# A second MLP layer on four column groups, stores of 16 rows, and five early loads issued by ScalarE

## The chip, the core and the metric

The kernel runs on one core of one Trainium2 chip. The metric is device time in microseconds; lower is better. Times are medians of several executions. Ratios are the mean time of one kernel's runs over that of the kernel before in the same rounds, so they are not quite the ratio of the medians quoted. A profile shows one execution, whose span (first to last instruction) is some 2 us shorter than its time. In profiles, PE is TensorE's matmuls, PEld its weight loads, DVE VectorE, ACT ScalarE, POOL GpSimd; SPq and ACTq are the DMA requests that SyncE and ScalarE issue.

## The reference

One decoding step of a transformer block for 8 batches: a conditioned layer norm, attention over a cache, and an MLP.

```python
B, Sq, D = (8, 1, 512);  Hq, Hkv, Sk, Dh = (32, 8, 8192, 128);  F = 1792      # bfloat16
mod = (silu(c) @ w_mod).reshape(B, 6, 1, D)          # sa, ca, ga, sb, cb, gb
h = layernorm(x) * (1 + ca) + sa
x = x + ga * (softmax(q(h) @ k_cache.T / sqrt(Dh)) @ v_cache @ wo)
h = layernorm(x) * (1 + cb) + sb
x = x + gb * (relu(h @ w1 + b1) ** 2 @ w2 + b2)
```

The two caches are 268 MB of the 284 MB that are read. All else is small.

## The kernel before

Keys and values come in 64 units of 4 MB (each two heads of one batch) through a ring of four slots. For each batch the order is units k0 to k3, then v0 to v3. A unit is requested when its slot has been read. All large loads are issued by SyncE, in one queue:

```python
d_wm = dma("sync", s_wm, ...)            # w_mod, 3 MB, ring slot 2
d_wq = dma("sync", s_wq, ...)            # wq, 4 MB, ring slot 3
...
load(0)
load(1)
dma("sync", s_bb, ...)                   # three small biases
...
d_wo = dma("sync", s_wo, ...)            # wo, 4 MB in rows of 4 KB
load(2)                                  # waits until w_mod has been read
load(3)                                  # waits until wq has been read
```

The request for unit 4 (the first values) also waits for wo, the output projection's weight, to have landed:

```python
def load(n):
    ...
    dep = [released.get(s), d_wo if n == NSLOT else None]
```

That wait guards the projection with wo. The projection stands inside the loop over batches and has no wait of its own for wo: it relies on some unit, asked for after wo landed, having been waited for earlier.

The end of the kernel, after the last values: first MLP layer, second layer with W2 stationary and 8 columns moving, scaling, transposing by matmul, copy, two stores of 8 rows of 512 B from neighbouring partitions:

```python
for f in range(FT):                      # 14 x 4 matmuls
    for k in range(KT):
        t = matmul(yT_ps[:, k, :], W2v[:, f, k * 128:(k + 1) * 128], hidT[:, f, :])
...
k_y2 = vector.tensor_tensor(y2T, yT_ps, mod(5), ALU.mult)
for cc in (1, 0):
    ...                                  # 2 matmuls by IDENT, then a copy into out_sb[rows, :]
    dma(("sync", "scalar")[cc], ..., outf[:, 256 * cc:256 * (cc + 1)], out_sb[rows, :])
```

Of the kernel before, what the change touches and what calls it, by code (L numbers as in the profile page):

```python
# [168 lines left out]
def bass_adaLN_cond__gqa_block_cached__dense_activation_squared_relu__decode_kernel(  # L169
# [10 lines left out]
    NSLOT = 4  # L180
# [6 lines left out]
    with ExitStack() as es:  # L187
# [25 lines left out]
        SEL = sb("SEL", [128, 4, 8], BF16)  # L213
# [13 lines left out]
        SELB = sb("SELB", [4, 4, B], BF16)  # L227
        SELP = sb("SELP", [128, B], FP32)
        x1T = sb("x1T", [128, KT, B], BF16)
# [4 lines left out]

        KF = KTb[:, :, :, :].rearrange("p a t r -> p (a t r)")
# [10 lines left out]
        EYEB = KF[:, 4544:4576].rearrange("p (g b) -> p g b", g=4)  # L246
# [5 lines left out]
        hidT = KF[:, 2560:2560 + FT * B].rearrange("p (f b) -> p f b", f=FT)  # L252
        out_sb = KF[:, 2048:2304]
# [4 lines left out]
        y2T = KF[:, 0:KT * B].rearrange("p (k b) -> p k b", k=KT)  # L258
# [38 lines left out]
        pool(lambda e: e.memset(IDF8[:], 0.0))  # L297
# [4 lines left out]
        pool(lambda e: e.memset(R4m[:], 0.0))  # L302
        pool(lambda e: e.memset(SEL[:], 0.0))
# [12 lines left out]
        t = select(IDF8[:], [[-1, 8]], 0, 1, 1.0, NE, t)  # L316
        k_id = t
        pool(lambda e: e.memset(KF[:, 4096:4096 + 64 * KT], 0.0))
        pool(lambda e: e.memset(EYE[:], 0.0))
        t = pool(lambda e: e.memset(EYEB[:], 0.0))  # L320
        t = select(EYE[:], [[-32, 4], [-1, B]], 0, 1, 1.0, NE, t)
        t = k_eye = select(EYEB[:], [[-32, 4], [-1, B]], 0, 1, 1.0, NE, t)
# [3 lines left out]
        for d in (-96, -64, -32, 0, 32, 64, 96):  # L326
            t = select(R4[:], [[-1, 128]], -d, 1, 1.0, NE, t)
        t = select(Qmask[:], [[-32, 4]], 0, 1, 0.0, GE, t)
        t = select(Qmask[:], [[32, 4]], 31, -1, 0.0, GE, t)
        for d in (0, 32, 64, 96):  # L330
            t = select(R4m[:], [[-1, 32]], -d, 1, 0.5, NE, t)

        for i in range(4):
            for cg in range(4):
                for half in range(2):
                    t = select(SEL[:, i, 4 * half:4 * half + 4], [[-1, 4]], -(32 * cg + 8 * i + 4 * half), 1,
                               1.0, NE, t)
# [5 lines left out]
        t = select(SELB[:], [[-1, 4], [0, B]], 0, 1, 1.0, NE, t)  # L343
# [11 lines left out]
        def load(n):  # L355
            kv, b, p = units[n]
            s = n % NSLOT
            src = (A_k_cache if kv == "k" else A_v_cache)[b, 2 * p:2 * p + 2]
            src = src.rearrange("g s d -> (g s d)").rearrange("(p f) -> p f", p=128)
            dep = [released.get(s), d_wo if n == NSLOT else None]  # L360
            if units[n] == last:
                t0, toks = 0, []
                for i, t1 in enumerate(CH):
                    toks.append(dma("sync", s_last[i - 1] if i else s_ring[s], lambda e, a=t0 * DH, z=t1 * DH: e.dma_start(
                        RING[:, s, a:z], src[:, a:z]), dep))
                    t0 = t1
                loaded[n] = toks
            else:
                loaded[n] = dma("sync", s_ring[s], lambda e: e.dma_start(slot(s), src), dep)
# [9 lines left out]
        k_csT = op("vector", lambda e: e.tensor_copy(csT[:, :, 0:B], csT_ps), [t, k_eye])  # L379
# [34 lines left out]
        k_mr1 = op("scalar", lambda e: e.activation(mod_r[:, 1, :], bank(1), ACT.Copy), [t])  # L414
# [8 lines left out]
        k_haT = op("vector", lambda e: e.tensor_tensor(haT[:, :, 0:B], tmpT[:], mod(0), ALU.add), [t])  # L423
        for i in range(KT):
# [7 lines left out]
               op("scalar", lambda e: e.activation(q_r[:, 1, :], bank(3), ACT.Copy), [t])]  # L432
        for u in range(2):
            for i in range(4):
                t = op("tensor", lambda e, u=u, i=i: e.matmul(
                    QT_ps[:, u, :, i, :], q_r[:, u, DH * i:DH * (i + 1)], EYEB[:, :, :]), [k_q[u]])
# [12 lines left out]
        k_cb1 = op("vector", lambda e: e.tensor_scalar(cb1[:], mod(4), 1.0, None, ALU.add))  # L449

# [3 lines left out]
        load(1)  # L454
        dma("sync", s_bb, lambda e: e.dma_start(
            b1_row[0:3, :], B_b1[0:128 * F2].rearrange("(o f) -> o f", o=3)), [k_brow])
        dma("sync", s_bb, lambda e: e.dma_start(
            b1_row[3:4, 0:256], B_b1[128 * F2:F].rearrange("(o f) -> o f", o=1)))
        d_bb = dma("sync", s_bb, lambda e: e.dma_start(b2_row, B_b2.rearrange("(o f) -> o f", o=4)))
        d_wo = dma("sync", s_wo, lambda e: e.dma_start(  # L460
# [56 lines left out]
        yT_ps = bank(2)[:, 0:KT * B].rearrange("p (k b) -> p k b", k=KT)  # L517

        def permute(pP, q0, q1, dst, deps, fill, then=None):
            n = q1 - q0  # L520
            for j in range(4):
                t = t_act = op("tensor", lambda e, j=j: e.matmul(
                    pP[:, j, 0:64 * n].rearrange("p (h x) -> p h x", h=2), PERM[:, j, :, :].rearrange("p h m -> p (h m)"),
                    oTn_p[:, :, q0:q1, :, :].rearrange("p h q r b -> p h (q r b)"), start=True, stop=True), deps)
            if fill:
                t_act = pe_stream(fill, 4)
# [3 lines left out]
            for hl in range(REP):  # L530
# [3 lines left out]
                if hl % 2:  # L534
                    toks.append(op("scalar", lambda e, dst=dst_h, frm=frm: e.activation(dst, frm, ACT.Copy), [t_act]))  # L535
# [13 lines left out]
        for b in range(B):  # L549
# [76 lines left out]
            for p in range(NP):  # L626
# [16 lines left out]
                if p == NP - 1:  # L643
                    proj_done = project(permute(
                        PS[:, 5:7, :].rearrange("p a (j c) -> p (a j) c", c=256), 0, 3, oPe,
                        [norm_last, k_all] + stg_free + hold, 3))
                    values(0, 16, 28)
                    Pg.at = "post" if lastb else (b, "b")
                if not lastu:
# [9 lines left out]
                    for i in range(4):  # L659
                        t = op("tensor", lambda e, i=i, osb=osb, oT_ps=oT_ps: e.matmul(  # L660
                            oT_ps, osb[:, i * 128:(i + 1) * 128], SEL[:, i, :], start=(i == 0), stop=(i == 3)),
# [12 lines left out]
                else:  # L674
# [29 lines left out]
                    for hh, (f0, n, a, z) in enumerate(((0, 4, 0, 2), (0, 4, 2, 3), (4, 2, 3, 4))):  # L704
                        for j in range(n):
                            op("tensor", lambda e, hh=min(hh, 1), f0=f0 + j, j=j, n=n, a=a, z=z: e.matmul(
                                hT_ps[hh][:, f0:f0 + 4 * (z - a - 1) + 1:4, 1, :], brow(j, n), SELB[:, a:z, :],
                                start=(f0 == 0), stop=False, skip_group_check=True), [d_bb, s_bank_free[min(hh, 1)]])
                    op("tensor", lambda e: e.matmul(
                        yT_ps, b2_row, SELB[:, :, :], start=True, stop=False, skip_group_check=True),  # L710
# [6 lines left out]
                    for i in range(4):  # L717
                        op("tensor", lambda e, i=i: e.matmul(
                            oT_ps, osb[:, i * 128:(i + 1) * 128], SEL[:, i, :], start=False, stop=False,
# [6 lines left out]
                    k_oP = permute(bank(6)[:, 0:256].rearrange("p (j c) -> p j c", c=64), 3, 4, oP, [t], 0,  # L726
# [10 lines left out]
        k_x1 = op("vector", lambda e: e.tensor_tensor(x1T[:], t1T[:], xT[:], ALU.add), [t])  # L737
        mean_ps = bank(3)[:, 0:B]
        for k in range(KT):
            t = op("tensor", lambda e, k=k: e.matmul(mean_ps, ONESMB[:, :], x1T[:, k, :], start=(k == 0),  # L740
                                                    stop=(k == KT - 1)), [k_x1])
        bc = lambda ap: ap.unsqueeze(1).to_broadcast([128, KT, B])
        t = op("vector", lambda e: e.tensor_tensor(xcT[:], x1T[:], bc(mean_ps), ALU.subtract), [t])
# [8 lines left out]
        for k in range(KT):  # L752
            if k == KT - 1:
                t = op("tensor", lambda e: e.matmul(var_ps, ONESM[:, :], sqs[:]), [k_sqs])
                t = op("scalar", lambda e: e.activation(std2[:], var_ps, ACT.Sqrt, bias=epst[:, 0:1]), [t])
                k_rstd = op("vector", lambda e: e.reciprocal(rstd2[:], std2[:]), [t])
            for f in range(FT):
                t = op("tensor", lambda e, f=f, k=k: e.matmul(
                    hT_ps[f // 8][:, f % 8, :, :], wcol(k, f), hbT[:, k, :, :], start=False, stop=(k == KT - 1),
                    skip_group_check=True), [k_hb, k_sb, d_w1[k // (KT - 1)]])  # L760
                if k == KT - 1 and f in (7, FT - 1):
                    hh = f // 8
                    fs = slice(8 * hh, f + 1)
                    t = op("vector", lambda e, hh=hh, fs=fs: e.tensor_tensor(
                        rT[:, fs, :], hT_ps[hh][:, :, 0, :], rsb(fs.stop - fs.start), ALU.mult), [t, k_rstd])
                    t = op("vector", lambda e, hh=hh, fs=fs: e.tensor_tensor(
                        rT[:, fs, :], rT[:, fs, :], hT_ps[hh][:, :, 1, :], ALU.add), [t])
                    k_sq.append(op("vector", lambda e, fs=fs: e.scalar_tensor_tensor(
                        hidT[:, fs, :], rT[:, fs, :], 0.0, rT[:, fs, :], ALU.max, ALU.mult), [t]))
        o_ps = bank(4)[:, 0:256]  # L770
        for f in range(FT):
            for k in range(KT):
                t = op("tensor", lambda e, f=f, k=k: e.matmul(  # L773
                    yT_ps[:, k, :], W2v[:, f, k * 128:(k + 1) * 128], hidT[:, f, :],
                    start=False, stop=(f == FT - 1), skip_group_check=True), [k_sq[f // 8], d_w2[f // 4]])
        for cc in range(2):
            for k in range(2):
                op("tensor", lambda e, k=k, cc=cc: e.matmul(
                    o_ps[64 * cc:64 * cc + B, 128 * k:128 * (k + 1)], x1T[:, 2 * cc + k, :], IDENT[:, :],
                    start=(k == 0), stop=False, tile_position=(0, 64 * cc), skip_group_check=True), [k_x1])  # L780
        k_y2 = op("vector", lambda e: e.tensor_tensor(y2T, yT_ps, mod(5), ALU.mult), [t])
        outf = out.rearrange("b s d -> (b s) d")
        d_o = []
        for cc in (1, 0):
            for k in range(2):
                t = op("tensor", lambda e, k=k, cc=cc: e.matmul(
                    o_ps[64 * cc:64 * cc + B, 128 * k:128 * (k + 1)], y2T[:, 2 * cc + k, :], IDENT[:, :],
# [40 lines left out]
```

## Time and profile before

| | kernel before |
|---|---|
| time | 669.41 us, median of 3 (668.55 to 670.22); 669.0 with a fourth run |
| span of the profile | 666.7 us |
| bytes read | 283.66 MB |
| busy: PE, DVE, ACT | 79%, 46%, 40% |
| one DMA queue | 99.3% of the span of 16 engines |

The prediction shows the rows of busy tenths and the queue's share. This is how the early requests look in the timeline of SyncE's queue. The columns are start and duration of the issuing instruction in us; "x2" merges neighbours, waits between them included, so such a duration is not that of one issue.

```profile
4.00 0.40 SPq L460 DMA_DIRECT2D wo_sb<-in_A_wo_dram  x1
14.86 23.69 SPq L369 DMA_DIRECT2D ring<-in_A_k_cache_dram  x2
51.38 31.83 SPq L369 DMA_DIRECT2D ring<-in_A_v_cache_dram  x4
```

### The profile page before, as it was taken

Reading aid. Unit: us, or ns where it says so; the run is one execution under the profiler, and the core shown is the slowest. Engines: PE = TensorE matmul, PEld = TensorE weight load, DVE = VectorE, ACT = ScalarE, POOL = GpSimd, SP = SyncE. Lnnn points to the kernel's source line nnn. Section 1 sums busy time; section 2 is a strip of 40 time slices with the busy share of each in tenths; the row PEclk is TensorE's granted clock in tenths of the full one; section 3 lists DMA queues with packets and bytes.
Section 4 is the critical chain, followed back from the end, with each engine's and each line's share of the span. In section 5 each row is a group of like instructions: output and inputs, shape, how many; then the busy total and the mean of one; then the engine's idle time right before and its main releaser. Section 6 shows DMA issues by size and latency. Waiting matters only on the chain.

```text
span 666.7 us, 15924 instructions
## 1 busy us (share of the span) xinstructions
PE 528.3 (79%) x7259; PEld 352.2 (53%) x7259; DVE 307.9 (46%) x587; ACT 264.3 (40%) x307; POOL 20.5 (3%) x79
## 2 busy tenths in 40 slices
PE   3494976898849987599858988499776998589887
PEld 2383732675328742477316753287424773277535
DVE  1262741466316652367415662167513673146633
ACT  2151631466115651166314661166512663146611
POOL 7400000000000000000000000000000000000000
PEclk9696998799969999699998999799997999879996
DMA  9999999999999999999999999999999999999997
GB/s 375 437 406 441 419 433 433 425 434 431 438 427 433 433 434 427 434 434 425 434 431 438 427 431 434 434 427 431 438 425 434 433 436 427 431 434 434 427 420 285
DMA packets 12189, 283.85 MB, mean 426 GB/s; under 512 B 1261, under 2 KB 1297, under 8 KB 3601
## 3 DMA queue, kind: packets, MB, share of 16 engines
q1 hardware_dynamic: 12128, 283.65, 99.3%
q8 instruction: 9, 0.15, 0.1%
q10 hardware_dynamic: 48, 0.02, 0.0%
q14 instruction: 4, 0.02, 0.0%
HBM read 283.66 MB, written 0.01 MB: 425 GB/s over the span
## 4 chain that ended last, share of the span: by engine, by line
PE 52%; DMA 38%; ACT 6%; DVE 2%; issue 1%; SPq 0%; DVEq 0%
PE PS L488 36%; DMA ring<-in_A_k_cache_dram 33%; PE PS L505 9%; ACT P_sb L582 5%; DMA ring<-in_A_v_cache_dram 4%; DMA ring<-in_A_wq_dram 2%; PE PS L636 2%; PE PS L478 1%; ACT KTb L493 1%; DVE O_sb L656 1%; PE PS L472 1%; PE PS L594 1%; DVE Pm L608 0%; PE PS L614 0%; PE PS L773 0%
## 5 line engine op out<-in xcount | busy, mean ns | idle before, releaser
L488 PE MATMUL PS<-IDENT,ring 128*128 128x128 bf16 x4096 | 267.1, 227 | 56.2 <-DMA ring<-in_A_k_cache_dram 56.2
L488 PEld LDWEIGHTS PS<-IDENT,ring 128*128 128x128 bf16 x4096 | 246.5, 102 | 104.8 <-DMA ring<-in_A_k_cache_dram 57.4
L493 ACT ACTIVATE KTb<-PS 128x1024 bf16<-128x1024 bf16 x192 | 196.5, 1024 | 236.6 <-PE PS L488 236.6
L495 DVE COPY KTb<-PS 128x1024 bf16<-128x1024 bf16 x320 | 210.0, 688 | 146.5 <-PE PS L488 144.4
L636 PE MATMUL PS<-ring,Pm 128*32 128x512 bf16 x1018 | 67.2, 409 | 24.8 <-DMA ring<-in_A_v_cache_dram 23.9
L505 PE MATMUL PS<-KTb,Qb 128*32 128x512 bf16 x1024 | 79.0, 385 | 4.5 <-ACT KTb L493 4.5
L656 DVE CAST O_sb<-PS 128x512 bf16<-128x512 f32 x31 | 21.5, 692 | 112.7 <-PE PS L636 112.7
L636 PEld LDWEIGHTS PS<-ring,Pm 128*32 128x32 bf16 x1018 | 26.5, 101 | 61.8 <-DMA ring<-in_A_v_cache_dram 33.7
L535 ACT ACTIVATE KTb<-PS 32x192 bf16<-32x192 f32 (+1 forms) x18 | 5.6, 310 | 110.0 <-PE PS L472 103.9
L582 ACT ACTIVATE P_sb<-PS,negm 128x1024 bf16<-128x1024 f32 x32 | 35.2, 1111 | 20.2 <-DVE negm L577 20.2
L478 PE MATMUL PS<-ONES 128*128 128x512 f32 x80 | 42.1, 630 | 0.0
L472 PE MATMUL PS<-IDENT 128*128 128x512 bf16 x112 | 33.4, 380 | 0.0
L594 PE MATMUL PS<-IDENT,P_sb 128*128 128x128 bf16 x256 | 19.9, 220 | 15.4 <-ACT P_sb L582 15.4
L608 DVE COPY Pm<-PS 64x512 bf16<-64x512 bf16 x48 | 20.2, 421 | 25.0 <-PE PS L594 24.5
L594 PEld LDWEIGHTS PS<-IDENT,P_sb 128*128 128x128 bf16 x256 | 14.4, 98 | 25.1 <-ACT P_sb L582 25.1
L505 PEld LDWEIGHTS PS<-KTb,Qb 128*32 128x32 bf16 x1024 | 15.4, 94 | 21.0 <-ACT KTb L493 8.5
L512 DVE TENSOR_REDUCE m<-PS 128x1 f32<-128x512 f32 x32 | 22.1, 689 | 6.6 <-PE PS L505 6.6
L660 PEld LDWEIGHTS PS<-SEL,O_sb 128*128 128x128 bf16 x124 | 5.8, 97 | 30.0 <-DVE O_sb L656 30.0
L478 PEld LDWEIGHTS PS<-ONES 128*128 128x128 f32 x80 | 12.7, 190 | 10.6 <-issue 10.6
L660 PE MATMUL PS<-SEL,O_sb 128*128 128x8 bf16 x124 | 7.8, 169 | 12.3 <-DVE O_sb L656 12.0
L472 PEld LDWEIGHTS PS<-IDENT 128*128 128x128 bf16 x112 | 9.9, 104 | 10.1 <-issue 7.2
L543 PE MATMUL PS<-wo_sb,KTb 128*32 128x512 bf16 x192 | 11.8, 380 | 3.3 <-ACT KTb L535 3.3
(134 smaller groups left out, 147.0 us busy)
## 6 DMA issues: line engine op xcount, KB each, us to landing
ring<-in_A_k_cache_dram SPq DMA_DIRECT2D x32, 4096.0 KB, 34.0
ring<-in_A_v_cache_dram SPq DMA_DIRECT2D x31, 4096.0 KB, 27.8
ring<-in_A_wq_dram SPq DMA_DIRECT2D x1, 4096.0 KB, 19.8
wo_sb<-in_A_wo_dram SPq DMA_DIRECT2D x1, 4096.0 KB, 47.3
ring<-in_w_mod_dram SPq DMA_DIRECT2D x1, 3072.0 KB, 10.5
ring<-in_A_v_cache_dram SPq DMA_DIRECT2D x1, 2048.0 KB, 22.5
ring<-in_B_w_dram SPq DMA_DIRECT2D x3, 512.0 KB, 19.2
ring<-in_B_w_dram SPq DMA_DIRECT2D x1, 1344.0 KB, 17.8
```

The costliest lines, as they stand in the source:

```text
L472: ts = [op("tensor", lambda e: e.matmul(bank(at).rearrange("p (a r) -> p a r", a=4), IDENT[:, :], rhs)) for _ in range(n)]
L478: ts = [op("tensor", lambda e: e.matmul(bank(at).rearrange("p (a r) -> p a r", a=4), ONES[:, :], rhs)) for _ in range(n)]
L488: t = op("tensor", lambda e, j=j, i=i: e.matmul(STG[j][:, i, :], src[:, 32 * k + 8 * j + i, :], IDENT[:, :], is_transpose=True), [loaded[n ...
L493: stg_free[j] = op("scalar", lambda e, j=j, dst=dst: e.activation(dst, STG[j], ACT.Copy), [t])
L495: stg_free[j] = op("vector", lambda e, j=j, dst=dst: e.tensor_copy(dst, STG[j]), [t])
L505: t = op("tensor", lambda e, hf=hf, q=q, rhs=rhs: e.matmul(PS[32 * q:32 * (q + 1), k, :], Qb[:, 2 * p + hf, :], rhs, start=(p == 0 and hf ...
L512: return op("vector", lambda e: e.tensor_reduce(m4[:, k:k + 1], bank(k), AX.X, ALU.max), [t])
L582: exps.append(op("scalar", lambda e, k=k: e.activation(P_sb[:, k, :, :, :], bank(k).rearrange("p (i x) -> p i x", i=8).unsqueeze(2).to_bro ...
L594: t = op("tensor", lambda e, k=k, i=i: e.matmul(STG[k][:, i, :], P_sb[:, k, i, :, :].rearrange("p h x -> p (h x)"), IDENT[:, :], is_transp ...
L608: done.append(op("vector", lambda e, dst=dst, frm=frm: e.tensor_copy(dst, frm), [t, k_pm]))
L636: t = op("tensor", lambda e, m=m, cg=cg, p=p, vt=vt, Obank=Obank: e.matmul(Obank[32 * cg:32 * (cg + 1), :], lhs[:, p, 32 * m:32 * m + 32], ...
L656: t = op("vector", lambda e, osb=osb, Obank=Obank: e.tensor_copy(osb, Obank), [t])
```

## The change

Intent: shorten the ending, by putting the output rows in the layout of the store without transposes; clear ScalarE of the early copies so that it can issue five early loads; and shorten the setup on GpSimd. The diff, cut to its core:

```diff
-            dep = [released.get(s), d_wo if n == NSLOT else None]
+            dep = [released.get(s), d_wo if n == 2 * NSLOT - 1 else None, k_wq if eng == "scalar" else None]
...
-        k_mr1 = op("scalar", lambda e: e.activation(mod_r[:, 1, :], bank(1), ACT.Copy), [t])
+        k_mr1 = op("vector", lambda e: e.tensor_copy(mod_r[:, 1, :], bank(1)), [t])
...
         load(0)
-        load(1)
-        dma("sync", s_bb, ...)                       # three biases
-        d_wo = dma("sync", s_wo, ...)
+        load(1, "scalar")
+        dma("scalar", s_bb, ...)                     # three biases
+        d_wo = dma("scalar", s_wo, ...)
...
-                    proj_done = project(permute(..., 3))
+                    t = permute(...)
                     values(0, 16, 28)
+                    proj_done = project(t)
...
-                    yT_ps[:, k, :], W2v[:, f, k * 128:(k + 1) * 128], hidT[:, f, :],
+                    y_ps[32 * k:32 * (k + 1), :], hidw[:, f].rearrange("p b r -> p (b r)"), W2v[:, f, k * 128:(k + 1) * 128],
+                    ..., tile_position=(0, 32 * k), ...
...
-        k_y2 = ...mult...; two transposes and a copy for each half; two stores of 8 rows of 512 B
+        t = op("vector", lambda e: e.tensor_tensor(y_sb, y_ps, mod5[:], ALU.mult), [t])
+        t = op("vector", lambda e: e.tensor_tensor(out_sb, y_sb, x1_sb, ALU.add), [t, k_res])
+        d_o = [dma(eng, s_out[h], lambda e, h=h: e.dma_start(
+            bass.AP(out.tensor, out.offset + 256 * h, [[128, 2], [D, B], [1, 128]]),
+            out_sb[64 * h:64 * (h + 1):4, :]), [t]) for h, eng in enumerate(("sync", "scalar"))]
```

Batch b of column group k now sits on partition 32k + 4b. So a store takes 16 rows of 256 B from every fourth partition. Because the wait for wo moved to unit 7, the projection had to move behind the first matmuls that wait for unit 7. ScalarE issues its five loads once wq has been read (`k_wq`), near 25 us.

## The prediction

> **What bounds the kernel now.** I read the page first, for its rows of busy tenths and of DMA queues, then the waits, then the timeline of the last microseconds, then the windows around the start and the end.
>
> The page, by 40 equal slices, with the totals of the queues:
>
> ```profile
> PE   3494976898849987599858988499776998589887
> DMA  9999999999999999999999999999999999999997
> GB/s 375 437 406 441 419 433 433 425 434 431 438 427 433 433 434 427 434 434 425 434 431 438 427 431 434 434 427 431 438 425 434 433 436 427 431 434 434 427 420 285
> q1 hardware_dynamic: 12128, 283.65, 99.3%
> HBM read 283.66 MB, written 0.01 MB: 425 GB/s over the span
> ```
>
> No compute engine is full (TensorE has slices at 3 to 5 tenths in every batch), but the transfers are: 9 in every slice but the last, 99.3% of the queue's time, some 433 GB/s in a steady slice. All 283.65 MB of the caches and weights go through one queue. 283.65 MB / 433 GB/s = 655 us; the start, the slower slices and what follows the last byte make up the other 12 us of a span of 666.7.
>
> The waits say the same from the other side. The engines wait for key and value data; the SyncE queue waits for buffers, and that idle costs nothing as long as requests are still outstanding:
>
> ```profile
> PE PS L488 <- DMA ring<-in_A_k_cache_dram: 56.2, 9, 9.9
> PEld PS L636 <- DMA ring<-in_A_v_cache_dram: 33.7, 15, 3.8
> SPq L116 <- DMA wo_sb<-in_A_wo_dram: 12.7, 1, 12.7
> ```
>
> Within a batch TensorE waits about 24 us for the next keys (chain of waits: 96.00 to 119.8, 173.04 to 197.5, and so on). So work inside a batch has about 24 us of slack each time.
>
> The tail, windows of the last stage and its timeline:
>
> ```profile
> 662.00:663.00 1.00, 0.87 (x34) 0.81 (x31) 0.21 (x1) 0.00 (x0) 0.00 (x0) 0.50 0.27 92
> 663.00:664.00 1.00, 1.00 (x27) 0.70 (x24) 0.19 (x1) 0.00 (x0) 0.00 (x0) 0.50 0.00 0
> ...
> 663.78 0.19 DVE L781 TENSOR_TENSOR KTb<-PS,modT 128x32 bf16<-128x32 f32 x1 [1.56 <-PE PS L773]
> 664.03 0.38 PE L786 MATMUL PS<-IDENT,KTb 128*8 128x128 bf16 x4
> 664.49 0.41 DVE L791 CAST KTb<-PS 8x256 bf16<-8x256 f32 x1 [0.51 <-PE PS L786]
> 664.92 0.31 SPq L794 DMA_DIRECT2D out_dram<-KTb  x1
> ```
>
> Bytes flow at 390 GB/s or more until 661 us and stop before 663. The last W2 piece was issued at 649.9 and took 13.5 us, so its landing is known at 663.4, and windows of 0.1 us show a short lull in the second layer's matmuls just there. So even the MLP at the end is paced by its weights. Only what comes after 663.4 is compute with nothing beside it: 663.4 to 666.7, 3.3 us.
>
> **What the Trainium skill says.** (1) "DMA: Bandwidth & Descriptors", section Issuing engines are not separate DMA queues: transfers issued by different engines run on the same 16 DMA engines and interleave. Here one queue carries all but 0.02 MB, so the trace cannot show it. It says that ScalarE's five issues buy no bandwidth. (2) The same page, section Queues, rings and completion order: each DMA engine takes turns between its queues packet by packet. No run yet has two busy queues; this is where my doubt lies. (3) "TensorE: Matmul & The Clock Gate", section Back-to-back issue gap: a matmul of N columns costs N/1.2 ns on the cold clock. It agrees: 32 matmuls of 512 columns on four column groups (L402, at clock 0.50) took 3.60 us; 8 rounds x 512/1.2 = 3.41, plus about 0.17 of latency. That also shows the four groups running together. (4) The DMA page's Specifications put 512 B as the smallest transfer at line rate; the new stores have rows of 256 B, the old 512 B. No run shows the cost yet.
>
> **The change part by part.**
>
> *Second MLP layer.* The 56 matmuls remain. Before, weights were stationary and 8 columns moved; two batches of them took about 1.02 and 0.94 us. After, the hidden vector is stationary and 128 columns of W2 move on four groups: at clock 0.5, 14 rounds x 107 ns = 1.49, plus 0.17, so 1.66 against some 2. But the layer waits for W2. After the last piece, 8 matmuls are left: before 663.35 to 663.76; after 2 x 0.107 + 0.17 = 0.38. Gain about 0.
>
> *Ending.* Before: scaling at 663.78, four transposing matmuls, a copy (0.41), stores at 664.85 and 664.92. After: a scaling of 128 columns from PSUM. A copy of 128x128 f32 from PSUM took 0.29 (L427) against 0.23 for 64 columns (L419), so I take 0.29; then an add in SBUF, estimated 0.25; two gaps of 0.03. The stores go out at 663.78 + 0.29 + 0.25 + 0.06 = 664.38, 0.54 us earlier. From issue to the end was 666.73 - 664.92 = 1.8 us, which I keep; 16 short rows may cost 0.1. Net gain 0.4 to 0.5 us.
>
> *First MLP layer.* Taking all of k for the first eight f before the rest brings the first hidden half about 0.8 us earlier (from 661.6 to about 660.8). W2 still lands at 663.4, so this is worth nothing.
>
> *Per batch.* The projection moves behind the first 16 value matmuls, three filler matmuls (0.81 us) go, and VectorE takes two copies of 0.34 us from ScalarE. The release of the last value slot moves by about the projection's 1.5 us. It frees room for a transfer whose data is needed over 20 us later. Zero.
>
> *Early copies and constants.* GpSimd loses some 40 selects (SEL's 32 took 10.3 us) and would end near 18 us in place of 29.4. But the first keys land at 30.8, so nothing waited for it long. Zero.
>
> *Early loads.* Before, SyncE queued 20 MB at once; the next request blocked for 22.6 us on a full queue. After, it queues w_mod, wq and unit 0 (11.5 MB, enough to 28 us); units 2 and 3 follow at 15 and 25 us, and at 25 us ScalarE adds unit 1, three biases and wo. Transfers never run dry there. Unit 0 is delayed to about 35 us and TensorE starts later, but gets through batch 0 sooner; the bytes are the same.
>
> What can cost time is the moved wait. SyncE must see wo landed before unit 7, no longer before unit 4. If turns go by single packets, a 4 KB packet of wo alternates with a 32 KB packet of keys. A DMA engine must move 64 packets of wo (64 x 0.16 = 10.2 us of its time) and sees only about 36 of SyncE's packets until unit 6 is done: four for half of unit 2 and eight each for units 3 to 6. Then 28 packets of wo run alone for 4.5 us, unit 7 is issued only when they have landed, and the engines idle from the last byte to the first of unit 7. From last byte to known landing is about 0.5 us (tail above); from issue to first data about 0.8 (issue at 0.80 us, and 77 GB/s over the first 2 us is 154 KB, 0.36 us at full rate). Together about 1.4 us, and the kernel, bound by transfers to the end, never wins it back.
>
> **The rivals.** A: *only the tail moves.* wo lands in time, transfers stay full: 669.41 - 0.5 = 668.9. For it: the change moves no bytes and the DMA row is full. B: *the moved wait opens a hole* in the first 110 us: 669.41 - 0.5 + 1.4 = 670.3. For it: the sizes of packets; against it: turns may be by larger packets, in which case wo is done near 60 us. C: *the start improves*: slice 3 has 406 GB/s, where the short packets of biases and wo begin; interleaved with long packets this may fill up, (433 - 406) x 16.7 us / 433 = 1.0 us, to 667.9. D: *ScalarE or SyncE is blocked by a full queue* while issuing wo, as SyncE was for 22.6 us; ScalarE's evictions would start late and unit 4 be asked for late, 672 to 675. Against it: wo was taken in 0.40 us behind more requests than ScalarE has.
>
> **Range and chances.** I give A 45%, B 35%, C 15%, D 5%: 0.45 x 668.9 + 0.35 x 670.3 + 0.15 x 667.9 + 0.05 x 673.5 = 669.5. I say 669.3, nearer to A. Three runs of before spread by 1.7 us, so the range is 667.3 to 671.6. Two per cent is 13.4 us; no mechanism here reaches it, except a long hole I have not seen. Faster 0.01, within 2% 0.97, slower 0.02.
>
> **What would show it.** In the new timeline the stores are issued about 0.5 us closer to the last scaling and no transposing matmuls stand between. Matmuls of the second layer still pause near the end for W2. The DMA row stays at 9; in A no 2 us window between 25 and 120 us drops under 400 GB/s for longer than before; in B one does around 95 to 105 us, with wo's landing just before unit 7's issue. In C slices 1 to 4 rise. I am wrong if the mean rate over the steady slices changes, if the key phase turns out bound by copies, or if the span moves by over 3 us either way.

## More of the kernel before

SyncE asks for wo at 4.00 us. It lands 47.3 us later (table of DMA issues), at 51.3, and the first value units are requested at once. At that moment units 2 and 3 are still queued, so the DMA engines never notice the wait.

## The result, and the profile after

The changed kernel took 672.27 us (median of 4, 671.9 to 672.44) against 669.0 in the same rounds: ratio 1.0045, interval 1.0028 to 1.0063. It is 3.3 us slower by the medians, within 2%, and 0.7 us above the top of the predicted range. All outputs are right.

The page of the changed kernel, same rows as the prediction showed:

```profile
DMA  9999989999999999999999999999999999999996
GB/s 374 435 428 430 423 357 408 436 438 438 424 426 432 438 438 424 430 430 436 438 430 428 430 432 438 438 424 426 432 438 438 424 426 432 438 438 426 428 418 262
q1 hardware_dynamic: 10930, 275.26, 95.7%
q10 hardware_dynamic: 1250, 8.41, 3.0%
```

The sixth slice (84 to 101 us) has 357 GB/s, the seventh 408; the kernel before had 433 in both. The queue of ScalarE (q10) now carries 8.4 MB, unit 1 and wo.

The same in three stretches, GB/s from the windows (a GB/s of rounding over 540 us is 1.3 us, so the last column alone cannot show a difference of 1 us):

| | 0 to 60 us | 60 to 120 us | 120 to 660 us |
|---|---|---|---|
| before | 410 | 430 | 431 |
| changed | 414 | 404 | 431 |

Between 60 and 120 us the changed kernel loses (430 - 404) x 60 / 430 = 3.6 us; it had gained (414 - 410) x 60 / 430 = 0.6 us ahead of that. Net some 3.0 us, all before 120 us.

Where exactly, by windows of the changed kernel (start:end, length, busy time and count of PE, PEld, DVE, ACT, POOL, then granted clock as a share of full speed, DMA share, GB/s; a packet is counted whole where it starts, hence the 524):

```profile
90.00:98.00 8.00, 7.09 (x80) 2.95 (x78) 2.02 (x5) 1.20 (x1) 0.00 (x0) 1.00 0.95 389
98.00:99.00 1.00, 1.00 (x21) 0.48 (x24) 0.00 (x0) 0.00 (x0) 0.00 (x0) 1.00 0.48 197
99.00:100.00 1.00, 1.00 (x21) 0.36 (x14) 0.00 (x0) 0.00 (x0) 0.00 (x0) 1.00 0.06 25
100.00:101.00 1.00, 0.95 (x9) 0.33 (x8) 0.69 (x1) 0.00 (x0) 0.00 (x0) 1.00 0.00 0
101.00:102.00 1.00, 0.80 (x8) 0.28 (x4) 0.20 (x2) 0.00 (x0) 0.00 (x0) 1.00 1.86 524
```

From 98 to 101 us the engines move 222 KB instead of 1290: a hole worth 2.5 us by this view. It has three parts, and the view shows only two. From 98.0 to about 99.6 some DMA engines are still at work and others have nothing left (by the kept trace, the 16 engines' shares of wo landed one after the other between 98.03 and 100.08 us); from 99.66, the end of wo's last packet, to 101.12 none moves a byte. The third comes after 101 us. The kept trace has every packet's start and duration; with its bytes spread over its duration, only 880 KB move from 101 to 104 us in place of 1290, because the engines start again unevenly too. By that count, 98 to 104 us lose 3.35 us.

The queue of SyncE says what it waited for. First its waits (total us, times, longest), then the timeline:

```profile
SPq L116 <- DMA wo_sb<-in_A_wo_dram: 29.3, 1, 29.3
```

```profile
100.16 0.33 SPq L359 DMA_DIRECT2D ring<-in_A_v_cache_dram  x1
100.53 1.48 SPq L359 DMA_DIRECT2D ring<-in_A_k_cache_dram  x3
```

For 29.3 us SyncE stood in front of unit 7 and waited for wo. Issued at 26.00 us, wo landed 74.1 us later. The packets of the kept trace show how. wo's first packet starts at 47.5 us, when unit 1, ahead of it in ScalarE's queue, is nearly through. From 49 to 93 us a DMA engine moves on average 34 packets of wo (4 KB) and 31 of SyncE's (32 KB), so nearly one for one. Then SyncE's run out (unit 6 has landed by 95.8 us), and wo's last 28 of 64 packets run alone. The three requests behind unit 7 (units 8 to 10) followed within 1.4 us of it: two of their slots had been free already.

The ending, by the timeline, to be set against the ending that the prediction shows:

```profile
667.33 0.29 DVE L773 TENSOR_TENSOR KTb<-PS,mod 128x128 bf16<-128x128 f32 x1 [2.61 <-PE PS L769]
667.66 0.23 DVE L774 TENSOR_TENSOR KTb<-KTb 128x128 bf16<-128x128 bf16 x1
667.91 0.68 SPq L775 DMA_DIRECT2D out_dram<-KTb  x1
667.91 0.65 ACTq L775 DMA_DIRECT2D out_dram<-KTb  x1
```

The scaling starts 3.55 us later than before (663.78), because the last bytes of W2 land 3.5 us later (666.83 against 663.33 in the kept traces). From there to the last issue it takes 0.58 us (before 664.92 - 663.78 = 1.14): 0.56 gained. From that issue to the end of the span it takes 670.7 - 667.9 = 2.8 us (before 1.8): 1.0 lost. Sum of the spans: 3.55 - 0.56 + 1.0 = 4.0, which is 670.7 - 666.7. (These are two single executions, of 672.44 and 668.45 us; the medians differ by 3.3.)

### The profile page after: what moved, and what is told of

It is laid out like the page before. It is cut to its first block, busy times and chain, and to the rows that moved or that the text cites. A ratio compares the mean times of both kernels' runs of the same rounds, so it can differ in the third digit from the quotient of the medians.

```text
span 670.7 us, 15780 instructions
## 1 busy us (share of the span) xinstructions
PE 529.2 (79%) x7231; PEld 351.2 (52%) x7231; DVE 316.3 (47%) x610; ACT 257.6 (38%) x288; POOL 13.4 (2%) x37
## 4 chain that ended last, share of the span: by engine, by line
PE 51%; DMA 34%; ACT 6%; another core or an unknown queue 4%; DVE 2%; SPq 1%; issue 1%
PE PS L482 36%; DMA ring<-in_A_k_cache_dram 29%; PE PS L499 9%; ACT P_sb L574 5%; DMA ring<-in_A_wq_dram 3%; DMA ring<-in_B_w_dram 3%; PE PS L628 2%; PE PS L472 1%; ACT KTb L487 1%; SPq L674 1%; DVE O_sb L648 1%; PE PS L466 1%; PE PS L586 1%; PE PS L392 1%
## 5 line engine op out<-in xcount | busy, mean ns | idle before, releaser
L628 PE MATMUL PS<-ring,Pm 128*32 128x512 bf16 x1018 | 69.7, 414 | 48.7 <-DMA ring<-in_A_v_cache_dram 47.6
L466 PE MATMUL PS<-IDENT 128*128 128x512 bf16 x88 | 26.9, 380 | 0.0
L652 PEld LDWEIGHTS PS<-R,O_sb 128*128 128x128 bf16 x124 | 5.7, 96 | 28.6 <-DVE O_sb L648 28.6
L535 PE MATMUL PS<-wo_sb,KTb 128*32 128x512 bf16 x192 | 18.8, 552 | 0.0
L652 PE MATMUL PS<-R,O_sb 128*128 128x8 bf16 x124 | 7.8, 169 | 12.4 <-DVE O_sb L648 12.0
L529 DVE CAST KTb<-PS 32x192 bf16<-32x192 f32 (+1 forms) x34 | 11.8, 346 | 6.1 <-PE PS L516 5.3
## 6 DMA issues: line engine op xcount, KB each, us to landing
wo_sb<-in_A_wo_dram ACTq DMA_DIRECT2D x1, 4096.0 KB, 74.1
```

What stands on the lines that cost most here:

```text
L466: ts = [op("tensor", lambda e: e.matmul(bank(at).rearrange("p (a r) -> p a r", a=4), IDENT[:, :], rhs)) for _ in range(n)]
L628: t = op("tensor", lambda e, m=m, cg=cg, p=p, vt=vt, Obank=Obank: e.matmul(Obank[32 * cg:32 * (cg + 1), :], lhs[:, p, 32 * m:32 * m + 32], ...
```

## The experiments

Theory H (hole): wo on ScalarE's queue gets few turns beside SyncE's large packets, lands late, and SyncE's wait before unit 7 leaves the DMA engines with nothing to do. Rival T: two queues in turn are slower in themselves. Rival S: the new stores make the loss. Rival L: the loss comes from unit 7 being late for TensorE.

The runs were made in three groups, each on one chip and beside its own runs of the kernel before, whose medians were 668.47 us (the first four runs below), 669.4 (wait at unit 4, repeat, and the first two of the stores) and 668.45 (the last two).

### wo issued by SyncE, nothing else

```diff
-        d_wo = dma("scalar", s_wo, lambda e: e.dma_start(
+        d_wo = dma("sync", s_wo, lambda e: e.dma_start(
```

> The changed kernel with one word different: SyncE, not ScalarE, issues wo (between units 0 and 2); unit 1 and the biases stay with ScalarE. Theory H (hole): wo on ScalarE's queue gets one 4 KB packet for each 32 KB packet of SyncE, lands at 100 us, and SyncE's wait for it before unit 7 empties the DMA engines, some 4 us. Then here wo lands near 50 to 60 us, windows from 90 to 110 us show 420 GB/s or more, and the time falls by 3 to 4 us against the changed kernel, to 668.5 to 669.5. Rival T (two queues in turn are slower in themselves): unit 1 still shares, most of the loss stays, 671 or more. Rival S (the new stores make the loss): nothing changes, 672.

Measured: 668.83 us (668.44 to 669.26), ratio to the kernel before 1.0002 (0.9988 to 1.0015). The three stretches have 410, 431 and 431 GB/s, as in the kernel before. The landing of wo, in the table of DMA issues (KB, us from issue to landing), and the windows:

```profile
wo_sb<-in_A_wo_dram SPq DMA_DIRECT2D x1, 4096.0 KB, 49.2
```

```profile
90.00:100.00 10.00, 8.62 (x93) 3.95 (x93) 3.11 (x9) 2.68 (x5) 0.00 (x0) 1.00 0.99 426
100.00:110.00 10.00, 4.04 (x46) 1.44 (x44) 2.30 (x6) 0.00 (x0) 0.00 (x0) 0.79 0.98 421
```

Issued at 2.19, wo lands at 51.4. One changed word takes away the whole loss. It also moves the issue of wo from 26.00 to 2.19 us; the run with wo first, below, separates the two. Unit 1 still shares the engines from ScalarE's queue, so T falls in its strong form; S falls as the main cause.

### Only the early issues, put into the kernel before

```diff
-            dep = [released.get(s), d_wo if n == NSLOT else None]
+            dep = [released.get(s), d_wo if n == 2 * NSLOT - 1 else None, k_wq if eng == "scalar" else None]
-        load(1); dma("sync", s_bb, ...) x3; d_wo = dma("sync", ...)
+        load(1, "scalar"); dma("scalar", s_bb, ...) x3; d_wo = dma("scalar", ...)
+                    proj_done = project(t)           # after values(0, 16, 28)
```

> The kernel before with only ScalarE's five early issues, the wait for wo moved to unit 7 and the projection behind the first value matmuls; ending, stores and early copies as before. Theory H: the same hole around 98 to 101 us, wo landing near 100 us, and time 671.5 to 672.5, that is +2.7 to +3.3 us on the kernel before. Rival S (the new ending and stores make the loss): 669, as before.

Measured: 672.41 us (672.02 to 672.51), ratio 1.0053 (1.0039 to 1.0067). Its windows, to be set against 333 and 367 GB/s in the changed kernel:

```profile
90.00:100.00 10.00, 9.09 (x113) 3.82 (x112) 1.97 (x5) 0.00 (x0) 0.00 (x0) 1.00 0.82 338
100.00:110.00 10.00, 2.34 (x15) 0.83 (x13) 1.59 (x4) 1.93 (x3) 0.00 (x0) 0.86 0.91 364
```

And wo took 74.1 us to land, just as in the changed kernel. So this part alone makes the loss, without the new ending and without the moved copies.

### Four stores of 8 rows in the changed kernel

```diff
-        d_o = [... two stores, [[128, 2], [D, B], [1, 128]] <- out_sb[64 * h:64 * (h + 1):4, :] ...]
+        for k in range(KT):
+            dma(("sync", "scalar")[k % 2], ..., outf[:, 128 * k:128 * (k + 1)], out_sb[32 * k:32 * (k + 1):4, :])
```

> The changed kernel with four stores of 8 rows of 256 B in place of two of 16 rows; two from each engine. If the longer ending comes from how a store of 2 x 8 rows is laid out over the DMA engines (issue 0.65 us, then later data), the issue takes 0.3 us each and the end comes 0.5 to 1.0 us sooner after the last add: 671.4. If rows of 256 B as such are slow, nothing is gained: 672.3 or a little more, for the second issue.

Measured: 673.23 us, ratio 1.0065 (1.0052 to 1.0079); a miss in the hoped direction. From the first issue to the end of the span it takes 671.4 - 668.0 = 3.4 us, against 2.8. The timeline, two stores merged on each engine:

```profile
667.98 1.49 SPq L778 DMA_DIRECT2D out_dram<-KTb  x2
667.99 1.54 ACTq L778 DMA_DIRECT2D out_dram<-KTb  x2
```

A store of 8 rows needs 0.64 to 0.80 us to issue here (about 0.75), no less than one of 16 rows (0.65 to 0.68).

### wo issued by ScalarE at the very start

```diff
+        d_wo = dma("scalar", s_wo, ...)          # right behind c and x
         d_wm = dma("sync", s_wm, ...)
...
-        load(1, "scalar")
+        load(1)
```

> The changed kernel with wo issued by ScalarE at the very start (right after c and x), unit 1 by SyncE, biases by ScalarE, the wait for wo still before unit 7. By theory H the 64 packets of wo per DMA engine need 64 packets of SyncE beside them, that is w_mod, wq and units 0 to 5; wo lands at 70 to 85 us, before unit 6's data ends, so there is no hole: 668.5 to 669.8. Rival T (two queues in turn are slower): as slow as the changed kernel or slower, 672 or more, since two queues are busy for longer.

Measured: 668.58 us (668.52 to 668.63), ratio 0.9997 (0.9984 to 1.0011), with the wait still in front of unit 7 and wo still on ScalarE's queue. Its landing in the table of DMA issues, and the window in which the changed kernel had 333 GB/s:

```profile
wo_sb<-in_A_wo_dram ACTq DMA_DIRECT2D x1, 4096.0 KB, 87.7
```

```profile
90.00:100.00 10.00, 5.89 (x62) 2.32 (x54) 1.77 (x4) 0.00 (x0) 0.00 (x0) 1.00 1.00 428
```

Here wo is even slower from issue to landing, 87.7 us, and shares the engines all that time; yet nothing is lost. So wo may stay on the second queue, if it is asked for early enough. It was issued at 1.79, lands at 89.5, and SyncE issues unit 7 at 89.55 (timeline of its queue), while unit 6 is still on its way. T falls, within the interval: two queues that take turns are not slower. The count of turns came out (when wo's last packet ends, at 87.7 us, SyncE's queue has moved 63 large packets per engine beside the 64 of wo); turned into time it gave 70 to 85 us, a few us too early. The absence of a hole holds.

### The wait moved back to unit 4, wo left with ScalarE

```diff
-            dep = [released.get(s), d_wo if n == 2 * NSLOT - 1 else None, k_wq if eng == "scalar" else None]
+            dep = [released.get(s), d_wo if n == NSLOT else None, k_wq if eng == "scalar" else None]
```

> The changed kernel with SyncE's wait for wo moved back to unit 4, as in the kernel before; wo stays with ScalarE. Theory H: the hole does not go but moves. SyncE has nothing queued behind unit 3 (done near 62 us), wo has sent some 16 of its 64 packets per DMA engine by then and the rest runs alone for 7 to 8 us, lands at 70 to 72 us, and units 4 and 5 go out then; a window there shows a hole, and the time stays within 0.7 us of the changed kernel, 671.5 to 672.7. Rival L (the loss comes from unit 7 being late for TensorE, not from idle DMA engines): the time returns to 669.

Measured: 672.62 us, ratio 1.0051 (1.0037 to 1.0064). The unaltered changed kernel beside it, a repeat:

> The changed kernel itself, unaltered, once more, so that the other runs have it beside them on the same chip. 671.5 to 672.5.

672.54 us, ratio 1.005 (1.0035 to 1.0066). The hole moved by 30 us, by the windows of the run with the wait at unit 4:

```profile
68.00:70.00 2.00, 2.00 (x37) 1.58 (x30) 1.30 (x3) 1.03 (x2) 0.00 (x0) 1.00 0.54 211
70.00:71.00 1.00, 1.00 (x18) 0.47 (x16) 0.81 (x2) 0.68 (x2) 0.00 (x0) 1.00 0.05 20
71.00:72.00 1.00, 1.00 (x21) 1.00 (x20) 0.48 (x1) 0.48 (x2) 0.00 (x0) 1.00 0.00 0
```

In these 4 us 442 KB move in place of 1720, a loss of 3.0 us by this view. The time in which nothing moves (70.88 to 72.34 us in the kept trace) is 1.46 us, the same as in the changed kernel. Because wo has only a handful of requests to share with before it is alone, it lands 44.9 us after its issue, at about 71 us, as H expected. TensorE is busy throughout this hole (1.00 of each us), so it is not TensorE's wait that costs the time: L falls. It is the idle DMA engines, wherever in the run they stand idle.

### The stores: row length, partition step, engines

Four runs look at the other term, the longer way from the issue of the store to the end. First, the kernel before with four stores of 8 rows of 256 B, from neighbouring partitions:

```diff
-            dma(("sync", "scalar")[cc], ..., outf[:, 256 * cc:256 * (cc + 1)], out_sb[rows, :])
+            for k in range(2):
+                dma(("sync", "scalar")[cc], ..., outf[:, 256 * cc + 128 * k:...], out_sb[rows, 128 * k:128 * (k + 1)])
```

> The kernel before with each of its two stores (8 rows of 512 B) cut into two of 8 rows of 256 B, from neighbouring partitions; so four stores of the shape of the four-store run, but with partition step 1, not 4. There each issue took 0.75 us. If rows of 256 B make a store slow to issue: about 0.75 us each here too, and the time rises by 1.2 to 1.6 us to about 670. If the step of 4 partitions does it: about 0.3 us each, and the time rises by only 0.3 us, to 668.8.

669.12 us, ratio 1.0008 (0.9994 to 1.0021). The timeline of the stores, two merged on each engine:

```profile
664.66 0.65 ACTq L795 DMA_DIRECT2D out_dram<-KTb  x2
664.74 0.68 SPq L795 DMA_DIRECT2D out_dram<-KTb  x2
```

Each issue takes 0.30 to 0.32 us, as with rows of 512 B (0.30). The same number, shape and length of rows took about 0.75 us from every fourth partition. So it is not the short row that makes the issue slow; the partition step is left, and the next run changes it in the new kernel.

Then that insight turned into a version: wo on SyncE and batches on neighbouring partitions (32k + b), four stores.

```diff
-        hidw = sb("hidw", [128, FT, B, 4], BF16)         # and x1w alike
+        hidw = sb("hidw", [128, FT, 4, B], BF16)
-            out_sb[64 * h:64 * (h + 1):4, :]
+            out_sb[32 * k:32 * k + B, :]                 # four stores
```

> The run with wo on SyncE, with the eight batches of a column group on neighbouring partitions (32k + b in place of 32k + 4b) and four stores of 8 rows. If the partition step made the stores slow: issues of 0.3 us, the end 2.1 us after the first issue, so 668.2 to 668.5, a little under the kernel before. If short rows or the number of stores do it: issues of 0.75 us and 3.4 us to the end, 669.5.

669.16 us, ratio 1.0000 (0.9987 to 1.0014): the issues came out, the time did not. The durations of the single issues (in ns: least, median, most):

```profile
L778 SPq DMA_DIRECT2D out_dram<-KTb x2: 309/340/372, 664.1 to 664.8; - x2
L778 ACTq DMA_DIRECT2D out_dram<-KTb x2: 302/308/315, 664.1 to 664.4; - x2
```

All four take 0.30 to 0.37 us, against 0.64 to 0.80 in the four-store run with its step of four partitions. So the step sets the issue time. Yet the end came 667.3 - 664.1 = 3.2 us after the first issue, not 2.1. Two things in this one profile account for it: SyncE starts its second issue 0.4 us after the first has ended, and seven of the eight DMA engines land that store by 666.10 us, the eighth at 666.80 (kept trace). What held either of them is not shown.

Third, both stores of 16 rows on SyncE; fourth, one store of 32 rows on SyncE (both with wo on SyncE and every fourth partition):

```diff
-            ...for h, eng in enumerate(("sync", "scalar"))]
+            ...for h, eng in enumerate(("sync", "sync"))]                                        # third
+        d_o = [dma("sync", ..., [[128, 4], [D, B], [1, 128]], out_sb[0:128:4, :])]               # fourth
```

> The run with wo on SyncE, with both stores of 16 rows issued by SyncE, one after the other. There each took 0.65 to 0.69 us to issue and the end came 2.5 us after. If the two stores hinder each other because both engines issue at the same moment: each issue takes 0.4 us or less here, and the end comes no later than 2.5 us after the first issue. If each is slow by itself (16 rows, partition step 4): 0.65 us each, and the end comes some 3.1 us after the first issue. In time 668.5 to 669.5, too close to tell; the timeline decides.

> The run with wo on SyncE, with a single store of all 32 rows of 256 B by SyncE. If the issue's time grows with the rows (8 rows of this partition step took 0.75 us, 16 rows 0.68 us): 0.7 us or not much more, and the end comes no later than with two stores, 2.5 us after the issue. If it is the two engines issuing at once that costs: 0.4 us and 2.1 us. 668.2 to 669.2.

The third: 669.52 us, ratio 1.0015 (0.9998 to 1.0031). Its issues took 0.68 and 0.52 us with 0.40 us between them, and the end came 3.3 us after the first: each is slow by itself, without the other engine. The fourth: 668.37 us, ratio 0.9997 (0.998 to 1.0014), its one store in the timeline:

```profile
664.13 0.70 SPq L775 DMA_DIRECT2D out_dram<-KTb  x1
```

Thirty-two rows cost one issue of 0.70 us and end 666.3 - 664.1 = 2.2 us after it, sooner than two stores at the same moment (2.5 with wo on SyncE) and than two in a row (3.3). So the issue time hardly depends on the number of rows (8, 16 and 32 rows at a step of four partitions: about 0.75, 0.68 and 0.70 us), and of the stores with this step the single one ended soonest. All these versions lie within 0.15% of the kernel before; none of them beats it beyond its interval.

## Why the prediction was wrong, point by point

- **What bounds the kernel: right.** Transfers decide. Where the DMA engines had work throughout (wo on SyncE, wo at the start) the time was that of the kernel before; where they lacked it for 3 us the time rose by 3 us, whatever TensorE did meanwhile.
- **Second MLP layer: right.** The layer pauses for W2 before and after (0.71 us in the last batch of matmuls after). With wo on SyncE the scaling starts at 663.69 us, before at 663.78; the new layout is worth nothing while W2 lands when it does.
- **Ending up to the issue: right.** Expected 0.60 us from scaling to the issue, measured 0.58.
- **"From issue to the end was 666.73 - 664.92 = 1.8 us, which I keep; 16 short rows may cost 0.1": wrong.** It was 2.5 us with wo on SyncE and 2.8 in the changed kernel. The length of the rows was not at fault. Issuing from every fourth partition takes 0.65 to 0.75 us in place of 0.3; by the kept traces the first row is on its way 1.27 us after the issue in place of about 0.8, and ScalarE's rows 0.28 us behind SyncE's, though both stores were issued at the same moment. In the changed kernel 0.3 us more passed after the last landing, which stays open. The store's 0.7 to 1.0 us ate the 0.56 us gained ahead of it.
- **Per batch, early copies and constants, first MLP layer: right.** With wo on SyncE all of them are in, and the ratio is 1.0002, with an interval of some 0.9 us either way; none was measured alone. But the reason given for the first, that TensorE waits about 24 us for the next keys in each batch, was a misreading. The 24 us are what a load of keys takes from issue to landing (96.00 to 119.8). The line shown beside it says what TensorE waited: 56.2 us in nine waits, the longest 9.9.
- **Rival B, the mechanism: right.** The count of packets (64 of wo against some 36 of SyncE's until unit 6 is done, the rest alone), the place (95 to 105 us) and the wait came out. In the trace SyncE's packets run out with 28 of wo's 64 left, the predicted number. I gave it 35% and put A, no hole, at 45%, for fear that turns might go by larger packets; if they did, wo would have landed near 60 us, not at 100. No run then had two busy queues and could tell.
- **Rival B, the size: "Together about 1.4 us": mis-sized, and this is the step that failed.** The idle time that it added up was right: from wo's last packet to the first new one it is 99.66 to 101.12, 1.46 us. What the sum left out is that sixteen engines neither stop nor start at one moment. By the packets of the kept trace they moved 259 KB in place of 690 between 98.0 and 99.6 us, 1.0 us, and 880 in place of 1290 between 101 and 104, another 0.95, of which 0.1 is still idle time. Together 3.35 us, more than twice the figure; with what was gained before 60 us, some 3 us net. The uneven stop could have been read from the prediction's own lines: between 662 and 663 us, before the last landing, the engines moved 92 GB/s and not 0 or 433.
- **Rival C: small.** The first 60 us gained 0.6 us at most, from 410 to 414 GB/s: slice 3 rose from 406 to 428, slice 4 fell from 441 to 430. Unit 0 landed at 32.7 us, not 35.
- **Rival D: no.** ScalarE issued its five loads between 24.65 and 26.40 us, each in 0.26 to 0.40 us, and was not blocked. (That a full queue held SyncE for 22.6 us in the kernel before is a reading; the trace shows only that this one issue lasted so long.)

Put together with the measured sizes: + 3.0 (hole and start) - 0.56 (ending) + 1.0 (stores) = + 3.4 us on 669.0, where 672.27 was measured. So the failed step is the size of the hole, 1.4 us where 3.35 was lost; next the end of the store, 1.8 to 1.9 us where it took 2.8; and the centre of the range leaned on A, in which there is no hole.

## What to carry to other kernels

In a kernel bound by transfers, ask of every wait in a queue of requests how many bytes are still queued behind it when it ends; if the awaited transfer is the last one under way, the engines stand partly or wholly idle for its uneven finish, its landing, the next start and the uneven restart (3.35 us here, of which only 1.46 was complete idleness). A transfer in small rows on a second queue beside large rows gets only a small share of the engines, so it lands late however early it seems to be issued: put it in the main queue in its proper place, or issue it so early that its share suffices. No run here took the wait out of SyncE's queue and gave it to the projection itself, which may be the simplest cure; it is untested. And an ending that saves instructions can lose it again in how the store is laid out over partitions.

## What the Trainium skill lacked or had wrong

- "DMA: Bandwidth & Descriptors", Queues, rings and completion order: it says an engine switches queues packet by packet, with typically 9 to 17 descriptors in a packet. Here the turns behave as if each row were a packet: from 49 to 93 us an engine moved 34 rows of wo (4 KB) and 31 of SyncE's (32 KB). wo (64 such rows for each of the 16 engines) took 74.1 us from issue to landing, of which it stood 21.5 behind unit 1 in its queue, and 87.7 us when issued at the start, where 10.2 us of engine time would do. By such turns a transfer of 4 KB rows gets one byte for eight of a transfer of 32 KB rows (an estimate from the row sizes, which fits the place of the hole); the page does not draw this.
- The same page has no time for the uneven finish and restart of the sixteen engines. Draining the queue and starting it again cost 3.35 us here (98 to 104 us): 1.0 us uneven finish, 1.46 us without a byte, 0.9 us uneven restart.
- The same page lacks that the partition step of a store sets its issue time: 0.30 to 0.37 us for 8 rows of 256 B from neighbouring partitions, 0.64 to 0.80 us from every fourth, 0.70 us for 32 rows from every fourth.
- The same page, Specifications, gives 512 B as the smallest transfer at line rate. For a store of 8 KB in all no cost of shorter rows was found: rows of 256 B in four stores instead of 512 B in two gave a ratio of 1.0008 (0.9994 to 1.0021).
- Two places agree with the runs. The same page, Issuing engines are not separate DMA queues: with wo at the start two queues were busy for over 80 us, and the time was neither better nor worse (ratio 0.9997). "TensorE: Matmul & The Clock Gate", Back-to-back issue gap, for small column groups too: 16 matmuls of 128 columns on four groups at clock 0.5 took 0.62 us in the second layer, against 4 x 128 / 1.2 = 0.43 us plus 0.17, which is what a matmul of 8 columns lasts in the trace.
